# The first block of an attention and feed-forward kernel: four tokens and then three, in place of three and four, with two ReLUs on the vector engine

## The chip, the cores and the metric

The kernel runs on one core of a Trainium2 chip. The metric is the device time of one execution in microseconds; the time of a kernel is the median of several executions. The engines are named as in the profile: PE multiplies matrices, PEld loads its weights, DVE is the vector engine, ACT the scalar (activation) engine, POOL the third elementwise engine, SP an engine that here only issues transfers. All engines take their own instructions in order and wait for one another through semaphores.

## The reference

The inputs are q, k and v, each of 8 batches, 12 heads, 448 positions and 64 values. Attention has a squared ReLU in place of the softmax, and its result goes through a normalised feed-forward layer:

```python
scores = scale * np.matmul(q, k.transpose(0, 1, 3, 2))
attn = np.maximum(scores, 0.0) ** 2 / S
attn_out = np.matmul(attn, v)
x = attn_out.transpose(0, 2, 1, 3).reshape(B, S, H * D)      # d_model = 768
xn = (x - mean(x)) / sqrt(var(x) + 1e-6) * g_ln
out = x + np.maximum(xn @ w_ch1, 0.0) @ w_ch2                # d_ff = 3072
```

## The kernel before

**Tiling.** The 448 positions of a batch are 64 rows of J = 7 positions each; a position within a row is called a token in this text, so one token is 64 columns. A batch is worked through in three groups (n = 0, 1, 2 for batch 0), each of two pairs of heads. Queries and keys are transposed by PE against an identity matrix (`piece`, L250), and DVE or ACT copies the result out of PSUM (L253).

**Blocks.** The queries of batches 0 and 1 are cut into two blocks of tokens, so that the feed-forward layer can start on the first block while attention works on the second. `BLK` (L131) gives the first token and the number of tokens of each block: (0, 3) and (3, 4) for batch 0, (0, 4) and (4, 3) for batch 1. `FEW` (L132) is the size of batch 0's first block. It also sets how the very first loads are cut (L188 to L191): the first FEW tokens of q and k, then the others, on the queues of SP and ACT.

**Scores.** `scores(n, slots, blk)` handles one or two key tokens ("slots") of group n against the block's queries: matmuls of quarter arrays into one PSUM tile (L365; four of them run side by side, each with as many columns as the block has tokens times 64), a ReLU of the tile to bf16 (L376), and a square that is put on the list `later`. `squares_now` (L354) issues the listed squares on DVE. A group has seven slots, so four calls: (0, 1), (2, 3), (4, 5) and (6). With four tokens a tile of two slots has 128 x 1024 elements, with three 128 x 768.

**Values.** `values(n, blk)` multiplies a group's squared scores with its values (L397, 28 matmuls) and DVE scales the sum out of PSUM (L403). `scaled` and `centre` multiply by g (L418, L420), sum over the model dimension on PE (L430), and subtract the mean (L437, six instructions). These tiles and those of the scores come from one pool of three PSUM buffers (`ps_sc`), taken in turn; two more (`ps_mm`) serve the feed-forward layer, fillers and transposes of batch 0.

**The order.** All of it is written out by hand. `first_block` (L549 onwards) runs the first block of batch 0 alone, with fillers (`busy`, `idle`) on PE. Then the feed-forward units of each block (`ffn1_head` L708, `ffn1` L682, each unit six matmuls over the weights w1) are issued between the attention units of the next block: batch 0's first block beside its second, that one beside batch 1's first, and so on. w1 arrives in twelve transfers that POOL issues (L177). `ffn1` gives its ReLU to ACT (L692) or DVE (L690). From about 89 us on come the last units of batch 1 and then the second layer and the other batches, in which no block is cut.

Of the kernel before, what the change touches and what calls it, by code (L numbers as in the profile page):

```python
# [8 lines left out]
ACTF = mybir.ActivationFunctionType  # L9
# [19 lines left out]
def kernel(  # L29
# [22 lines left out]
    nc = tc.nc  # L52
# [9 lines left out]
    J = S // HP  # L62
# [47 lines left out]
    def slots_of(pool, kind, shape, n, o):  # L110

        size = shape[0] * shape[1]
        made = [pool.tile([P, *shape], bf16, tag=f"{kind}{i}", name=f"{kind}_sb", bufs=1) for i in range(n)]
        return made + [spare[:, o:o + size].rearrange("p (a b) -> p a b", b=shape[1])]

    slots = {
        "k": slots_of(io, "k", (2, S), 2, 0),
        "v": slots_of(io, "v", (2, S), 3, 2 * S),
        "kT": slots_of(tpool, "kT", (J, P), 2, 4 * S),
        "qT": slots_of(tpool, "qT", (NB, P), 2, 6 * S)}  # L120
# [7 lines left out]
            return slots[kind][n % 3 if n < LATE else n % 2]  # L128
        return slots[kind][0 if n == G else (n - 2) % 3 if n < LATE else (n + 1) % 2]

    BLK = (((0, 3), (3, J - 3)), ((0, 4), (4, J - 4)))  # L131
    FEW = BLK[0][0][1]  # L132


# [87 lines left out]
    def scale_g():  # L222
        for hf in range(2):
            nc.tensor.matmul(
                idle_ps[hf * HP:(hf + 1) * HP, 1, :K1], g_rows[:, hf], identity_g,
                start=True, stop=True)
        nc.vector.tensor_copy(g_sb, idle_ps[:, 1, :K1])
        nc.vector.tensor_scalar_mul(g_mean, g_sb, -1.0 / d_model)
# [12 lines left out]
    def piece(sb, b, m, n, lo, hi, bank=True):  # L241

        if b == 0 and bank:
            ps = ps_mm.tile([P, 1024], bf16, tag="mm", name="tr_ps")
        else:
            ps = ps_sc.tile([P, 2, 1024], bf16, tag="sc", name="tr_ps")[:, 0]
        src, i = qkv[n, b, m], "qk".index(n)
        for j in range(lo, hi):
            for pr in range(2):
                nc.tensor.transpose(  # L250
                    ps[pr * HP:(pr + 1) * HP, j * P:(j + 1) * P],
                    src[:, pr, j * D:(j + 1) * D], identity)
        return lambda copy, lo=lo, hi=hi: copy(  # L253
            sb[:, i * J + lo:i * J + hi, :], ps[:, lo * P:hi * P].rearrange("p (j c) -> p j c", c=P))
# [76 lines left out]
    FULL = (0, J)  # L331
    FIRST, LAST = (0, BLK[0][0]), (1, BLK[1][1])
    n_early = [0]

    def busy(n):


        ps = ps_mm.tile([P, 512], fp32, tag="mm", name="busy_ps")
        for _ in range(n):
            nc.tensor.matmul(ps[:, :P], ones, ones, start=True, stop=True)  # L340
# [7 lines left out]
    def squares_now(n=None, but=0):  # L348

        if n is None or n in [k for k, _ in later]:
            for _, a in later[:len(later) - but]:
                nc.vector.tensor_mul(a, a, a)  # L354
            del later[:len(later) - but]

    def scores(n, slots, blk, act=False):
        g, w = st[groups[n]], blk[1] * HP
        ps = ps_sc.tile([P, 2, 512], fp32, tag="sc", name="sc_ps")
        for o, i in enumerate(slots):  # L360
            for r in range(2):
                rows = slice(r * HP, (r + 1) * HP)
                for hh in range(2):
                    cols = slice(hh * HP, (hh + 1) * HP)
                    nc.tensor.matmul(  # L365
                        ps[cols, r, o * w:(o + 1) * w], g["k"](i)[rows, cols],
                        g["q"](i, r)[rows, blk[0]:sum(blk), cols], start=True, stop=True)
        if groups[n][0]:
            a = apool.tile([P, 2, 512], bf16, tag="attn", name="attn_sb")
        else:  # L370
            o = n_early[0] % 12 * 1024
            a = early[:, o:o + 1024].rearrange("p (r s) -> p r s", r=2)
            n_early[0] += 1
        since[0] = 0
        a = a[:, :, :len(slots) * w]
        nc.scalar.activation(a, ps[:, :, :len(slots) * w], ACTF.Relu)  # L376
        if act:
            nc.scalar.activation(a, a, ACTF.Square)  # L378
        elif blk == FULL:
            nc.vector.tensor_mul(a, a, a)  # L380
        else:
            later.append((n, a))
        for o, i in enumerate(slots):
            g["attn"].append(a[:, :, o * w:(o + 1) * w])

    def values(n, blk):
        squares_now(n)
        b, m = groups[n]
        v_sb, g, w = qkv["v", b, m], st[groups[n]], blk[1] * HP
        ps = ps_sc.tile([P, 2, 512], fp32, tag="sc", name="av_ps")  # L390
        for j in range(J):
            for hh in range(2):
                rows = slice(hh * HP, (hh + 1) * HP)
                for pr in range(2):
                    cols = slice(pr * HP, (pr + 1) * HP)
                    i, r = g["where"](pr, j)
                    nc.tensor.matmul(  # L397
                        ps[cols, hh, :w], v_sb[rows, pr, j * D:(j + 1) * D],
                        g["attn"][i][rows, r, :], start=(j == 0), stop=(j == J - 1))
        if b // 2 not in xT:  # L400
            xT[b // 2] = xpool.tile([P, K1, S2], bf16, tag="xT", name="xT_sb")
        x = xT[b // 2][:, 2 * m:2 * m + 2, of(blk, b)]
        nc.vector.tensor_scalar_mul(x, ps[:, :, :w], score_scale)  # L403
        g["attn"] = []
        since[0] = 9
        if blk == FULL:
            return
        if b not in xc:
            xc[b] = x_room[:, b]
        if (b, blk) != FIRST:  # L410
            scaled(b, m, blk)

    def scaled(b, m, blk):

        for c in range(2 * m, 2 * m + 2):
            x, y = xT[b // 2][:, c, of(blk, b)], xc[b][:, c, of(blk)]
            if (b, blk) == FIRST:
                nc.scalar.mul(y, x, g_sb[:, c:c + 1])  # L418
            else:
                nc.vector.tensor_scalar_mul(y, x, g_sb[:, c:c + 1])  # L420
# [82 lines left out]
    def transposed(n):  # L503

        if groups[n][0] < by_dma:
            transposes(*groups[n])
            return


        if by_dma * G < n < LATE:  # L510
            load(n + 2, "kq")
        keys_dma(n)
        queries_dma(n)
        if n == LATE + 1:
            put_off.append((n + 2, "kq"))
        elif n >= LATE:
            load(n + 2, "kq")
# [31 lines left out]
    def first_block():  # L549

        blk, sb = BLK[0][0], None
        transposed(0)
        sb = st[0, 0]["sb"]
        scores(0, (0, 1), blk)
        piece(sb, 0, 0, "k", FEW, J)(nc.vector.tensor_copy)
        scale_g()
        busy(3)
        for i in (2, 4, 6):  # L560
            squares_now()
            scores(0, tuple(range(i, min(i + 2, J))), blk)
            busy(3)
        transposed(1)
        squares_now()
        scores(1, (0, 1), blk)
        scores(1, (2, 3), blk)
        busy(3)
        transposed(2)
        squares_now()  # L570
        scores(1, (4, 5), blk)
        held.pop()()
        scores(1, (6,), blk)
        squares_now()
        values(0, blk)
        scores(2, (0, 1), blk)
        busy(3)
        scores(2, (2, 3), blk)
        busy(3)
        scores(2, (4, 5), blk)  # L580
        squares_now(but=2)
        values(1, blk)
        squares_now()
        scores(2, (6,), blk)
        (_, last), = later
        later.clear()
        nc.scalar.activation(last, last, ACTF.Square)
        scaled(0, 0, blk)
        piece(sb, 0, 0, "q", FEW, J, False)(nc.scalar.copy)
        scaled(0, 1, blk)  # L590
        busy(6)
        values(2, blk)
        scaled(0, 2, blk)
        centre(0, blk)
# [586 lines left out]
    def ffn1_units(b, blk):  # L1181
        if (b, blk) == LAST:
            return ([lambda: ffn1_head(b, blk)]
                    + [lambda ni=ni: ffn1_two(b, ni, blk) for ni in range(3, K2 - 1, 2)]
                    + [lambda: ffn1(b, K2 - 1, blk)])
        return [lambda: ffn1_head(b, blk)] + [lambda ni=ni: ffn1(b, ni, blk) for ni in range(3, K2)]
# [36 lines left out]
    pairs = B // 2  # L1223
    narrow = ctx.enter_context(ExitStack())
    first_block()


    units, side = ffn1_units(0, BLK[0][0]), attention_block(0, BLK[0][1])
    units, late = units[:-4], units[-4:]
# [12 lines left out]
    load(8, "qk")  # L1242
    units = ffn1_units(0, BLK[0][1])
    interleave(units[:1] + late + units[1:], attention_block(1, BLK[1][0]), 3)
    fold_tiles()
# [155 lines left out]
```

## Time and profile before

| what | value |
|---|---|
| time, median of 3 runs | 514.17 us (513.85 to 514.24) |
| the profiled execution's own time | 514.53 us |
| its span in the profile | 512.7 us |
| PE busy | 504.5 us, 98% of the span |
| DVE busy | 387.3 us, 76% |
| ACT busy | 309.4 us, 60% |
| POOL busy | 129.6 us, 25% |

Times within the profile count from the start of the span. A line of a timeline or a chain gives the start, the busy time, the engine and the source line, what is written and read, and how many instructions were merged; in brackets it gives the engine's idle time before and what ended it. "sc_ps" are PSUM tiles of scores, "av_ps" of values, "h_ps" of the feed-forward layer, "tr_ps" of transposes; "early" is the room in SBUF in which batch 0's transposed queries and keys and its scores lie. A busy PE is modelled to the end of each matmul's passage through the array, so short idle times of the array do not show.

The early part of the kernel in marks from the trace: the first transposes at 4.60 us, the first scores at 6.07, the first matmul of the feed-forward head of batch 0's first block at 19.51, that of its second block at 37.64, of batch 1's first block at 66.56.

### The profile page before, as it was taken

To read this page: it belongs to the slowest core of one execution; us is meant where nothing else is said; L and a number is where in the kernel's file an instruction comes from. 1 tells how busy PE (TensorE), PEld (TensorE's weight loads), DVE (VectorE), ACT (ScalarE), POOL (GpSimd) and SP (SyncE) were. 2 spreads that over 40 slices of the span, in tenths; PEclk is the share of its full clock that TensorE was granted. 3 is DMA by queue.
4 is the path that set the end of the run, shared out by engine and by line. 5 is a ranking of instruction groups with operands and counts; after the bars stand their busy time and mean duration, and the time that the engine had idled before them with its cause. 6 is when DMAs were issued, how large, how long until landed. Compare 5 with 4: busy or idle time off the path is not lost.

```text
span 512.7 us, 11440 instructions
## 1 busy us (share of the span) xinstructions
PE 504.5 (98%) x4553; PEld 299.0 (58%) x4553; DVE 387.3 (76%) x745; ACT 309.4 (60%) x496; POOL 129.6 (25%) x182
## 2 busy tenths in 40 slices
PE   8899999999999999999999999999999999999996
PEld 6677788855555555555555555555555555556663
DVE  5775765389899888858789968858887968868663
ACT  5966676488678266657757266639979366630000
POOL 8335112012301266321201099501100022200000
PEclk9999999999999999999999999999999999999999
DMA  9999999999969985329995989304997393322222
GB/s 196 206 207 206 211 206 159 158 145 185 190 141 166 185 197 175 130 65 168 187 245 106 186 186 184 94 11 84 188 185 173 71 215 124 94 77 63 63 61 61
DMA packets 124486, 76.31 MB, mean 149 GB/s; under 512 B 80562, under 2 KB 120498, under 8 KB 124434
## 3 DMA queue, kind: packets, MB, share of 16 engines
q1 hardware_dynamic: 93730, 41.38, 39.6%
q0 software_dynamic: 28544, 30.91, 38.3%
q10 hardware_dynamic: 2160, 3.31, 2.8%
q8 instruction: 35, 0.57, 0.5%
q14 instruction: 17, 0.14, 0.1%
HBM read 64.69 MB, written 17.89 MB: 161 GB/s over the span
## 4 chain that ended last, share of the span: by engine, by line
PE 94%; ACT 2%; DVE 1%; DMA 1%; issue 1%; SPq 0%; DVEq 0%
PE m_ps L899 28%; PE o_ps L741 20%; PE o_ps L1109 9%; PE m_ps L1109 8%; PE h_ps L682 8%; PE sc_ps L365 8%; PE av_ps L397 6%; PE h_ps L726 2%; PE h_ps L708 2%; PE o_ps L1071 2%; ACT early L376 1%; PE tr_ps L250 1%; DMA stage_sb<-in_q_dram 1%; DMA out_dram<-o_room 1%; DVE o_room L1125 0%
## 5 line engine op out<-in xcount | busy, mean ns | idle before, releaser
L376 ACT ACTIVATE attn_sb<-sc_ps 128x896 bf16<-128x896 f32 (+4 forms) x150 | 126.3, 902 | 39.4 <-PE sc_ps L365 34.5
L903 ACT ACTIVATE hT_sb<-m_ps 128x448 bf16<-128x448 f32 x144 | 78.2, 543 | 52.0 <-PE m_ps L899 49.3
L741 PE MATMUL o_ps<-w,hT_sb 128*128 128x384 bf16 x624 | 108.3, 327 | 0.0
L741 PEld LDWEIGHTS <-hT_sb 128*128 128x128 bf16 x624 | 58.2, 98 | 45.7 <-issue 10.1
L380 DVE TENSOR_TENSOR attn_sb<-attn_sb 128x896 bf16<-128x896 bf16 x98 | 61.7, 645 | 19.8 <-ACT attn_sb L376 19.1
L682 PE MATMUL h_ps<-x_room,w 128*128 128x256 bf16 (+2 forms) x384 | 43.8, 263 | 0.4 <-ACT early L376 0.3
L1109 PEld LDWEIGHTS <-hT_sb 128*128 128x128 bf16 x312 | 29.7, 98 | 22.1 <-issue 3.0
L980 DVE TENSOR_TENSOR m_ps<-x_room,m_ps 128x448 f32<-128x448 f32 x36 | 22.6, 629 | 23.8 <-ACT hT_sb L903 23.6
L682 PEld LDWEIGHTS <-w 128*128 128x128 bf16 x384 | 33.8, 97 | 7.2 <-issue 2.8
L899 PEld LDWEIGHTS <-w 128*128 128x128 bf16 x246 | 23.9, 97 | 23.1 <-issue 0.4
L1109 PEld LDWEIGHTS <-x_room 128*128 128x128 bf16 x252 | 24.2, 98 | 17.4 <-issue 1.6
L403 DVE TENSOR_SCALAR xT_sb<-av_ps 128x896 bf16<-128x896 f32 (+2 forms) x30 | 27.0, 901 | 9.3 <-PE av_ps L397 9.2
L964 ACT COPY x_room<-m_ps 128x448 f32<-128x448 f32 x36 | 19.1, 531 | 21.6 <-PE m_ps L899 20.7
L899 PEld LDWEIGHTS <-w_sum 128*128 128x128 bf16 x210 | 20.5, 98 | 19.1
L159 POOL DMA_DIRECT2D k_sb<-in_k_dram x15 | 10.7, 712 | 81.1 <-DMA kT_sb<-k_sb 57.3
L899 PE MATMUL m_ps<-x_sum,w 128*128 128x448 bf16 x120 | 29.1, 352 | 0.1
L659 DVE BATCH_NORM_STATS2 stats<-xtok_sb 128x6 f32<-128x384 bf16 x56 | 28.3, 548 | 0.0
L159 POOL DMA_DIRECT2D v_sb<-in_v_dram x20 | 14.2, 711 | 55.5 <-PE sc_ps L365 40.7
L365 PE MATMUL sc_ps<-qT_sb,kT_sb 64*64 64x448 bf16 x392 | 28.2, 358 | 0.0
L692 ACT ACTIVATE hT_sb<-h_ps 128x256 bf16<-128x256 f32 (+1 forms) x49 | 18.0, 368 | 16.1 <-PE h_ps L682 15.2
L378 ACT ACTIVATE attn_sb<-attn_sb 128x896 bf16<-128x896 bf16 x28 | 26.6, 950 | 0.9
L397 PE MATMUL av_ps<-attn_sb,v_sb 64*64 64x448 bf16 (+2 forms) x532 | 26.2, 331 | 0.1
(196 smaller groups left out, 871.7 us busy)
## 6 DMA issues: line engine op xcount, KB each, us to landing
out_dram<-o_room SPq DMA_DIRECT2D x108, 96.0 KB, 2.8
w<-in_moe_w_ch_dram POOLq DMA_DIRECT2D x12, 384.0 KB, 14.3
w<-in_moe_w_ch_dram POOLq DMA_DIRECT2D x4, 1152.0 KB, 20.0
q_sb<-in_q_dram POOLq DMA_DIRECT2D x20, 224.0 KB, 6.2
v_sb<-in_v_dram POOLq DMA_DIRECT2D x20, 224.0 KB, 6.6
k_sb<-in_k_dram POOLq DMA_DIRECT2D x15, 224.0 KB, 6.0
kept<-room SPq DMA_DIRECT2D x4, 480.0 KB, 2.6
kept<-w_sum SPq DMA_DIRECT2D x16, 96.0 KB, 1.7
```

Source lines behind the costliest of these rows:

```text
L365: nc.tensor.matmul(ps[cols, r, o * w:(o + 1) * w], g["k"](i)[rows, cols], g["q"](i, r)[rows, blk[0]:sum(blk), cols], start=True, stop=True)
L376: nc.scalar.activation(a, ps[:, :, :len(slots) * w], ACTF.Relu)
L378: nc.scalar.activation(a, a, ACTF.Square)
L380: nc.vector.tensor_mul(a, a, a)
L397: nc.tensor.matmul(ps[cols, hh, :w], v_sb[rows, pr, j * D:(j + 1) * D], g["attn"][i][rows, r, :], start=(j == 0), stop=(j == J - 1))
L403: nc.vector.tensor_scalar_mul(x, ps[:, :, :w], score_scale)
L659: nc.vector.bn_stats(stats[:, n], xtok[pair][:, n * G:(n + 1) * G, t, :])
L682: nc.tensor.matmul(ps[:, :w + more], w1[:, c, ni * P:(ni + 1) * P], xc[b][:, c, s.start:s.stop + more], start=(c == 0), stop=(c == K1 - 1))
L741: nc.tensor.matmul(ps[:, :DH], hT[pair][:, ki, t * P:(t + 1) * P], w2[:, ki, cols], start=(o == 0), stop=(o == K2 - 1))
L899: nc.tensor.matmul(ps, *at, start=(first and c == 0), stop=(c == KQ - 1), skip_group_check=not first)
L903: nc.scalar.activation(hT[pair][:, n + KH * row, half * S:(half + 1) * S], ps, ACTF.Relu)
L1109: nc.tensor.matmul(ps, x[:, ki], y[ki] if isinstance(y, list) else y[:, ki], start=(first and ki == 0), stop=(ki == KH - 1), skip_group_ch ...
```

## The change

Batch 0's blocks become (0, 4) and (4, 3), the same as batch 1's, and `FEW` with them becomes 4. `scores` gets a parameter with which DVE does the ReLU in place of ACT. `first_block` uses it twice: for slots 4 and 5 of group 0, and for slot 6 of group 1. Line numbers behind L376 move by three.

```diff
-    BLK = (((0, 3), (3, J - 3)), ((0, 4), (4, J - 4)))
+    BLK = (((0, 4), (4, J - 4)), ((0, 4), (4, J - 4)))
     FEW = BLK[0][0][1]
...
-    def scores(n, slots, blk, act=False):
+    def scores(n, slots, blk, act=False, dve=False):
...
         a = a[:, :, :len(slots) * w]
-        nc.scalar.activation(a, ps[:, :, :len(slots) * w], ACTF.Relu)
+        if dve:
+            nc.vector.tensor_scalar_max(a, ps[:, :, :len(slots) * w], 0.0)
+        else:
+            nc.scalar.activation(a, ps[:, :, :len(slots) * w], ACTF.Relu)
...
         for i in (2, 4, 6):
             squares_now()
-            scores(0, tuple(range(i, min(i + 2, J))), blk)
+            scores(0, tuple(range(i, min(i + 2, J))), blk, dve=i == 4)
             busy(3)
...
         held.pop()()
-        scores(1, (6,), blk)
+        scores(1, (6,), blk, dve=True)
         squares_now()
         values(0, blk)
         scores(2, (0, 1), blk)
```

With the new FEW, the first loads of q and k hold four tokens (256 KB each) and the second ones three (192 KB each); in the first block every tile of scores, values, sums and feed-forward outputs of batch 0 is a third wider, and in its second block a quarter narrower. The number of instructions stays the same.

## The prediction

> **What bounds the kernel now.** First the page: the chain of waits by engine, and the busy slices of PE.
>
> ```profile
> PE   8899999999999999999999999999999999999996
> PE 94%; ACT 2%; DVE 1%; DMA 1%; issue 1%; SPq 0%; DVEq 0%
> ```
>
> PE sets the end, except in the first three slices of 12.8 us. Once PE never waits, a delay at the start is a delay at the end, unless PE later waits less or has less to do. So I sum over PE: waits added less waits removed. The windows view places them (columns: length, busy us of PE, PEld, DVE, ACT, POOL, granted clock, DMA share, GB/s).
>
> ```profile
> 4.60:10.20 5.60, 5.01 (x95) 3.31 (x95) 3.42 (x10) 4.15 (x7) 5.57 (x9) 1.00 1.26 215
> 10.20:14.90 4.70, 4.01 (x109) 3.03 (x110) 4.03 (x11) 4.04 (x7) 1.97 (x3) 1.00 1.26 204
> 14.90:19.50 4.60, 4.04 (x104) 3.01 (x104) 2.98 (x8) 4.57 (x11) 1.90 (x3) 1.00 1.24 207
> 21.90:26.10 4.20, 3.85 (x66) 2.86 (x65) 3.24 (x9) 3.76 (x6) 1.37 (x2) 1.00 1.24 207
> 37.60:66.50 28.90, 28.90 (x444) 22.62 (x443) 18.96 (x41) 19.10 (x38) 9.58 (x13) 1.00 1.19 209
> ```
>
> The first block ends at 19.5. In its three windows ACT is 74, 86 and 99% busy, DVE 61, 86 and 65%; PE's 85 to 89% contain fillers that compute nothing. From 37.6 PE is full. The chain in order of time shows who leads in the first block, and where PE waits after it:
>
> ```profile
> 9.83 0.37 DVE early L253
> 10.24 0.61 PE sc_ps L365 x16
> ...
> 12.37 0.81 ACT early L376
> 13.18 0.48 ACT early L253
> 13.66 2.53 ACT early L376 x4
> ...
> 17.98 0.57 DVE xT_sb L403
> ...
> 19.51 2.03 PE h_ps L708 x18
> ```
>
> Copies of transposed keys on DVE release group 1's scores (10.24); then ACT's ReLUs lead to 16.2; a DVE copy leads into the centring. Both engines' queues matter, and the change moves work from one to the other while widening everything. After 19.5 PE has three waits over 0.25 us:
>
> ```profile
> 22.55 0.95 PEld L682 LDWEIGHTS <-w 128*128 128x128 bf16 x12 [0.33 <-issue]
> ...
> 26.12 0.96 PE L397 MATMUL av_ps<-early,v_sb 64*64 64x256 bf16 x28 [0.28 <-ACT early L376]
> ...
> 30.23 0.66 PE L682 MATMUL h_ps<-x_room,w 128*128 128x192 bf16 x6 [0.32 <-ACT early L376]
> ```
>
> The prices, from groups by form (count, busy us, mean ns):
>
> ```profile
> L403 DVE TENSOR_SCALAR xT_sb<-av_ps 128x896 bf16<-128x896 f32 x18 | 19.5, 1086 | 2.6 <-PE av_ps L397 2.6
> L403 DVE TENSOR_SCALAR xT_sb<-av_ps 128x512 bf16<-128x512 f32 x6 | 4.1, 691 | 2.7 <-PE av_ps L397 2.6
> L354 DVE TENSOR_TENSOR early<-early 128x1024 bf16<-128x1024 bf16 x9 | 5.9, 684 | 0.0
> L354 DVE TENSOR_TENSOR early<-early 128x768 bf16<-128x768 bf16 x9 | 4.7, 553 | 0.5 <-ACT early L376 0.4
> L376 ACT ACTIVATE early<-sc_ps 128x1024 bf16<-128x1024 f32 x9 | 8.8, 1019 | 0.7 <-PE sc_ps L365 0.6
> L376 ACT ACTIVATE early<-sc_ps 128x768 bf16<-128x768 f32 x9 | 6.9, 816 | 1.6 <-PE sc_ps L365 1.6
> ```
>
> A ReLU of 1024 on DVE out of PSUM has no row. By the two L403 rows (same form of operation, same source) an element costs (1086-691)/384 = 1.03 ns, so it takes 1.22 us; below it lies the 0.69 of 512, above it 1.37 (twice 0.69). I take 1.22. One of 512 takes 0.69. Work queued back to back starts about 0.09 us before the one ahead has ended (the timeline's starts and ends on DVE; 0.10 on ACT).
>
> **The change part by part.**
>
> *First loads, four tokens in place of three (L191).* q landed at 4.18 and k at 4.52. Bounds: no shift, and in proportion to size, a third of 3.4 us (192 KB took 3.4 and 3.8 us to land, 256 KB 4.3 and 4.6). Between 4.52 and 5.88 another 512 KB landed, 0.34 us for 128 KB; so k +0.34 and q half of it. The other half's loads shrink by as much and land when they did. Cast of k on ACT 0.51 to 0.62, two more transposes and a wider copy (0.36 to 0.42): first scores +0.45, at 6.5.
>
> *Group 0, and DVE's first ReLU.* Two ReLUs of 1019 on ACT from 6.95 end at 8.98, so the square of slots 2, 3 starts at 9.03 (before 8.47). Behind it on DVE: that square (0.68), the new ReLU (1.22), its square (0.68), and only then the key copy that frees group 1's scores: 9.03 + 0.60 + 1.26 + 0.60 + 0.36 = 11.85 (the ReLU with its 0.04 handover). Before, that copy ended at 10.19. The ReLU taken from ACT saves nothing here: ACT had 0.74 us idle before 10.66. Scores of group 1: +1.65, at 11.9. PE's transposes of group 1 are done by then, nothing else is queued on it, and it waits. This is the largest term.
>
> *Groups 1 and 2.* ACT's three ReLUs of group 1 are 0.20 wider each and lose a 0.20 wait: the third ends +2.05, at 15.2. DVE's second ReLU (0.69, slot 6) stands ahead of two squares and of the copy of group 0's values, which frees a PSUM buffer for group 2's slots 4, 5. That copy ended at 14.91. Now DVE runs without a break from the key copies of group 2 (11.68 + 1.6 = 13.3), start to start: copies 0.54 and 0.27, squares 0.60 and 0.60, ReLU 0.60, squares 0.60 and 0.33, the copy itself 0.69: 17.5. So those scores come +2.55. Wider ReLUs and ACT's square (0.2+0.1+0.1+0.1): +3.05 when the last square ends. Values (28 matmuls, 0.19 more), scaling, column sums: the FFN head (L708) starts +3.5, at 23.0; its pace is set by six wider L437 (410 to 479 ns by form), so it ends some +3.95.
>
> *Work that only moved.* 18 matmuls of 256 columns took 1.97 us in the chain, of 192 1.50: 26 ns for 64 columns; a quarter-array one 6.8 (28 took 0.77 and 0.58). Scores and values 168 x 6.8 = 1.14, sums 6 x 26 = 0.16, head 18 x 26 = 0.47: 1.75 us that block two no longer does. So the added wait is 3.95 - 1.75 = **+2.2**.
>
> *Waits that go.* The 0.33 names no engine; weights issued near 9.5 and landing 9.3 to 15.0 us later fit it, and the stage now comes 3.5 us later. The 0.28 and 0.32 are for ReLUs of 1024, now 768 (0.2 less each), behind units 0.16 longer. **-0.9**; bounds -0.5 and -1.3 (with handovers too small for rows).
>
> *Batch 1's first block* (37.6 to 66.5) keeps ReLUs of 1024, but the FFN units between them shrink to 192 columns: 12 matmuls, 0.31 us less per step. At 55 to 60 ACT was 4.62 of 5.00 us busy, and PE's values take the PSUM buffer that a ReLU frees. Two steps have that little room: 0 to +0.6, I take **+0.2**.
>
> *POOL and SP.* POOL's cast of the other query half narrows (0.66, a quarter fewer elements), so the w issues come at most 0.13 earlier into transfers that already share 204 to 215 GB/s: nothing, bounds -0.1 and 0. SP and ACT issue the same four loads.
>
> Sum: +2.2 - 0.9 + 0.2 = **+1.5 us**. The profiled execution took 514.53 (span 512.7), 0.36 over the median; the sum puts it at 516.0, span 514.2, and the median at 515.7.
>
> **Rivals.** (1) *Half of it hides:* DVE's ReLU nearer to ACT's pace (1.02) and later small waits closing bring +0.6, 514.8. For: handovers below 0.1 us are many. Against: the DVE rows are dense and linear. (2) *The other side, faster:* 10 to 37 us is paced by the w transfers (DMA share 1.24 to 1.26 in every window), and PE merely has to be ready as they land. Then the 2.2 is covered, wider tokens give each weight more work, and all handover waits go: up to -1.1, 513.1. It decides if the next block's head (L708, at 37.64) comes less than 1 us later. Against: only one PE wait in that stretch names no engine. (3) *ACT takes over in batch 1:* PE waits at each of three groups for 0.3 to 0.4 us, +1.0 above the forecast, 516.7. For: 4.62 of 5.00. (4) *PE's clock falls back* in the longer waits at 10 and 16 us. At the start 30 fillers took 3.38 us, 113 ns each; six later ones took 0.44, 73 ns. A second slow phase as long as the first (1.1 to 5.4), with PE some four fifths busy, costs up to 2: 1.7, 517.4. Against: the waits are under 2 us, with matmuls between them. That the change does not do what it says is excluded by the built order: DVE holds the two ReLUs.
>
> By the Trainium skill (TensorE: Matmul & The Clock Gate, "What's actually happening") the array falls to half clock after an idle window of about 3.4 us. By that rule the waits here are too short and rival 4 fails; the trace shows two speeds of fillers, while its granted clock reads 1.00 throughout.
>
> **How the numbers follow.** Forecast 0.55 (its own range 514.9 to 516.5), rivals 0.18, 0.09, 0.14, 0.04. What a measurement can tell from no change is 0.2%, 1.03 us: 513.14 to 515.20. Slower: 0.51 of the forecast with rivals 3 and 4, 0.69; faster: rival 2 and 0.01 of rival 1, 0.10; same: what is left of the forecast (0.04) and of rival 1 (0.17), 0.21. From 514.3 to 516.9 leaves out rivals 2 and 4 and the ends of 1 and 3, under 0.2.
>
> **What would show it.** First scores near 6.5; an idle PE before group 1's scores (about 11.9, released by DVE's copy); FFN head near 23.0; no PE wait over 0.25 us from 23 to 41; the next heads near 41.4 and 68.0 in place of 37.64 and 66.5. It is wrong if group 1's scores start before 11, or if the lag of 3.5 us at the first head is not near 1.5 at batch 1's second block.

## The result, and the profile after

| | before | after |
|---|---|---|
| time, median of 4 runs each | 514.04 us (513.85 to 514.24) | 518.20 us (517.73 to 518.36) |
| ratio, 95% interval | | 1.0065 (1.0042 to 1.0088) |
| the profiled execution's own time | 514.53 us | 517.73 us |
| its span | 512.7 us | 515.9 us |
| PE busy | 504.5 us | 506.4 us |

The changed kernel is slower by 4.2 us, and the forecast of 515.7 and its range (up to 516.9) were both too low. The page of the changed kernel, PE's slices, the granted clock's slices, and the chain by engine:

```profile
PE   8899999999999999999999999999999999999996
...
PEclk9999999999999999999999999999999999999999
...
PE 93%; DVE 3%; ACT 1%; issue 1%; DMA 1%; DVEq 0%
```

DVE has 3% of the chain in place of 1%, and PE 93% in place of 94%. In these coarse slices nothing else shows, and the granted clock stands at 9 (90% or more) from the first slice on. The windows of the changed kernel, with the columns used before:

```profile
4.60:10.20 5.60, 5.01 (x60) 2.74 (x61) 2.57 (x7) 3.12 (x4) 5.42 (x9) 1.00 1.26 217
10.20:14.90 4.70, 4.24 (x81) 3.17 (x83) 3.85 (x8) 2.28 (x5) 2.04 (x5) 1.00 1.26 205
14.90:19.50 4.60, 3.41 (x89) 2.44 (x87) 4.60 (x9) 4.23 (x5) 1.93 (x3) 1.00 1.24 206
...
24.70:43.00 18.30, 18.30 (x278) 14.52 (x278) 13.47 (x35) 12.37 (x24) 8.38 (x12) 1.00 1.25 205
43.00:69.60 26.60, 25.92 (x445) 21.23 (x442) 17.94 (x40) 18.35 (x39) 5.72 (x8) 1.00 1.17 210
```

The first line holds the finding. From 4.6 to 10.2 us PE was busy for 5.01 us, to the hundredth as long as before, but it got through 60 matmuls in place of 95. The tiles are only a third wider, and not all of them, so this is more than the change itself explains. The rest is in the timeline of the changed kernel (start, busy us, engine, line, what is written and read, count):

```profile
1.09 3.38 PE L236 MATMUL idle_ps<-ones 128*128 128x128 bf16 x30 [1.09 <-DVE ones L98]
...
4.59 0.46 DVE L199 CAST q_sb<-stage_sb 128x512 bf16<-128x512 f32 x1 [0.99 <-DMA stage_sb<-in_q_dram]
...
5.10 0.64 PE L250 MATMUL tr_ps<-identity,q_sb 128*64 128x128 bf16 x8 [0.63 <-DVE q_sb L199]
...
10.90 1.22 DVE L377 TENSOR_SCALAR early<-sc_ps 128x1024 bf16<-128x1024 f32 x1
10.91 0.50 PE L340 MATMUL busy_ps<-ones 128*128 128x128 bf16 x3
...
13.96 0.34 PE L340 MATMUL busy_ps<-ones 128*128 128x128 bf16 x3
```

Three fillers are the same instruction throughout, 128 columns on constants, with no input to wait for. They take 0.50 us at 10.91 and 0.34 at 13.96. In the kernel before, the change comes much earlier (timeline, same columns):

```profile
5.55 0.34 PE L236 MATMUL idle_ps<-ones 128*128 128x128 bf16 x3
...
6.92 0.34 PE L340 MATMUL busy_ps<-ones 128*128 128x128 bf16 x3
```

In the single records, neighbouring 128-column matmuls start 107 ns apart ahead of the change and 56 ns apart behind it. So PE begins every profiled execution at about half its speed and changes over once. I call that moment the **speed-up**, and read it from the spacing of the records: 5.5 us before, 12.7 us after. The mean granted clock does not show the slow phase, because the record that it is taken from, which lies in the packed traces, begins only at the speed-up: at 5.50 us before, at 12.69 after.

The chain of the changed kernel (start, us, what) shows what stood on the path meanwhile:

```profile
6.76 0.64 PE sc_ps L365 x8
...
11.41 1.55 PE tr_ps L250 x28
...
12.98 0.37 DVE early L253
13.40 0.63 PE sc_ps L365 x16
...
16.95 0.60 DVE early L377
17.55 0.94 DVE early L354 x2
18.49 0.61 DVE xT_sb L406
...
24.66 1.45 PE h_ps L711 x10
```

From group 1's scores on the chain goes where the prediction said, through DVE's second ReLU, squares and copy to group 2. Ahead of them it does not: the copy that releases them (12.98) was to wait for DVE's first ReLU and its square, but the chain reaches it through PE's own transposes of group 1, which run at half speed and end at 12.96. DVE's first ReLU is not on this chain. Group 1's scores come at 13.40 (before 10.24, forecast 11.9) and the head L711 (the old L708) at 24.66 (before 19.51, forecast 23.0). The three later heads lie at 43.09, 69.61 and 90.44 us, and the first matmul of L729, the part behind the last units of batch 1, at 91.94; before, it lay at 88.82. I call this last one **the mark**. From it to the end of the span both took 423.9 us, so that the 3.1 us by which it moved are the 3.1 us of the span. (The medians differ by 4.2 us because the profiled execution of before lay 0.5 us above its median and that of after was the fastest of its four.)

### The profile page after: what moved, and what is told of

Same layout as the page of the kernel before. It is cut to its first block, busy times and chain, and to the rows that moved or that the text cites. A ratio compares the mean times of both kernels' runs of the same rounds, so it can differ in the third digit from the quotient of the medians.

```text
span 515.9 us, 11434 instructions
## 1 busy us (share of the span) xinstructions
PE 506.4 (98%) x4553; PEld 300.6 (58%) x4553; DVE 390.2 (76%) x747; ACT 308.7 (60%) x494; POOL 129.5 (25%) x182
## 4 chain that ended last, share of the span: by engine, by line
PE 93%; DVE 3%; ACT 1%; issue 1%; DMA 1%; DVEq 0%
PE m_ps L902 27%; PE o_ps L744 20%; PE o_ps L1112 10%; PE m_ps L1112 8%; PE sc_ps L365 7%; PE h_ps L685 7%; PE av_ps L400 6%; PE h_ps L729 2%; PE o_ps L1074 2%; PE h_ps L711 1%; ACT attn_sb L379 1%; PE tr_ps L250 1%; DMA stage_sb<-in_q_dram 1%; DVE xT_sb L406 1%; DVE early L354 1%
## 5 line engine op out<-in xcount | busy, mean ns | idle before, releaser
L1112 PEld LDWEIGHTS <-x_room 128*128 128x128 bf16 x252 | 24.2, 98 | 17.3 <-issue 1.6
L695 ACT ACTIVATE hT_sb<-h_ps 128x256 bf16<-128x256 f32 (+1 forms) x49 | 17.9, 366 | 15.6 <-PE h_ps L685 15.0
```

The lines of the kernel that those rows point to most:

```text
L1112: nc.tensor.matmul(ps, x[:, ki], y[ki] if isinstance(y, list) else y[:, ki], start=(first and ki == 0), stop=(ki == KH - 1), skip_group_ch ...
```

## The experiments

Theory **C**: the sum of the prediction holds for an execution with an early speed-up, and the rest of the loss is PE's half speed lasting longer. Rival **W**: the waits in DVE's and ACT's queues are longer than reckoned, whatever PE's speed. After the first four runs C was sharpened to **C2**: PE's speed-up varies from execution to execution, and comes later when PE has idle time among its first matmuls. In the diffs, idle(n) issues n fillers ahead of the first data, and busy(n) fillers between attention steps. Edits are against the changed kernel unless "before" is named. The kernel before ran beside each set of experiments, with medians of 514.30 (a to d), 514.36 (e to h), 514.19 (i, j) and 514.33 us (k, l).

All profiled executions in one table (us from the span's start; "scores 1" are the first scores of group 1):

| kernel | speed-up | first scores | scores 1 | first head | mark | span |
|---|---|---|---|---|---|---|
| before | 5.5 | 6.07 | 10.24 | 19.51 | 88.82 | 512.7 |
| after | 12.7 | 6.76 | 13.40 | 24.66 | 91.94 | 515.9 |
| a: after, 36 fillers | 4.3 | 6.48 | 11.99 | 23.25 | 90.53 | 514.4 |
| b: before, 25 fillers | 3.9 | 5.68 | 9.94 | 19.21 | 88.33 | 512.3 |
| c: new blocks, ACT's ReLUs, 36 | 7.1 | 6.63 | 11.40 | 22.34 | 89.61 | 513.5 |
| d: old blocks, DVE's ReLUs | 6.0 | 6.13 | 10.88 | 20.40 | 89.33 | 513.2 |
| e: after again | 13.6 | 7.33 | 14.07 | 25.32 | 92.58 | 516.5 |
| f: after, slot 6 alone on DVE, 36 | 5.9 | 6.57 | 11.14 | 22.39 | 89.66 | 513.6 |
| g: after, 36, more fillers in group 0 | 6.2 | 6.69 | 12.36 | 23.62 | 90.89 | 516.0 |
| h: before, 33 fillers | 4.0 | 5.54 | 10.00 | 19.26 | 88.35 | 512.4 |
| i: before, 12 fillers | 15.6 | 5.87 | 12.35 | 22.92 | 91.85 | 516.6 |
| j: new blocks, ACT's ReLUs, 30 | 16.7 | 6.75 | 13.49 | 25.73 | 93.01 | 516.7 |
| k: after a third time | 17.3 | 6.72 | 13.46 | 25.91 | 93.18 | 516.9 |
| l: as j | 12.5 | 7.05 | 13.46 | 24.40 | 91.67 | 516.2 |

### a: the changed kernel with six more fillers at the start

```diff
-            idle(30)
+            idle(36)
```

> The changed kernel with 36 fillers on PE at the start in place of 30, so that PE works on until the later queries arrive (5.1 us). Theory C (the clock): the forecast of +1.5 us was right about waits, and the other 1.6 us come from PE running at half speed until 12.6 us in place of 5.5, because it stood idle for 0.8 us before the first transposes; with the gap filled PE should speed up near 5.5 us, first scores near 6.6, group 1's scores near 11.9, the FFN head near 23.1, and the time should fall to about 516.6 us. Theory W (waits only; the slow phase is a matter of chance or covered by waits): the time stays within 0.5 us of 518.2.

Measured: 517.27 us (516.27 to 517.84, 6 runs), ratio 1.0048 (1.0032 to 1.0064). The median lies between the theories. The profiled execution was the fastest of the six, 516.27, and had its speed-up at 4.3 us; from its timeline:

```profile
7.32 0.34 PE L340 MATMUL busy_ps<-ones 128*128 128x128 bf16 x3
...
9.72 1.22 DVE L377 TENSOR_SCALAR early<-sc_ps 128x1024 bf16<-128x1024 f32 x1
...
10.97 0.69 DVE L354 TENSOR_TENSOR early<-early 128x1024 bf16<-128x1024 bf16 x1
...
11.58 0.94 DVE L253 COPY early<-tr_ps 128x384 bf16<-128x384 bf16 x3
11.99 0.63 PE L365 MATMUL sc_ps<-early 64*64 64x256 bf16 x16 [1.68 <-DVE early L253]
```

With PE at full speed the first block behaves as forecast. DVE's ReLU of 1024, its square and the key copies stand one behind the other, PE is idle for 1.68 us waiting for them, and the scores come at 11.99 (forecast 11.9). The heads lie at 23.25, 41.68 and 68.19 (forecast 23.0, 41.4, 68.0) and the span is 514.4 (forecast 514.2). Between this execution and that of the changed kernel above lie 13.40 - 11.99 = 1.41 us at scores 1, 24.66 - 23.25 = 1.41 at the first head, 69.61 - 68.19 = 1.42 at the third and 91.94 - 90.53 = 1.41 at the mark. All of it arises before scores 1, while one of the two runs at half speed, and none afterwards. (This is against a speed-up at 4.3, which is earlier than the 5.5 of before; what that is worth is taken up in the part on the prediction.) The other five executions were slower, four of them by 0.9 us or more, so six fillers do not secure an early speed-up.

### b: the kernel before with five fillers fewer

```diff
 (the kernel before)
-            idle(30)
+            idle(25)
```

> The kernel before with 25 fillers at the start in place of 30: PE idles some 0.8 us ahead of the first transposes, as in the changed kernel, and nothing else differs. Theory C: PE stays at half speed past 5.5 us, to 9 or 12.6 us, and the time rises by 0.4 to 1.9 us (514.5 to 515.9). Theory W: no change within 0.3 us.

Measured: 516.32 us (514.13 to 517.58, 12 runs), ratio 1.0032 (1.0017 to 1.0047). Instructions that compute nothing, ahead of all data, cost 2.0 us at the median when taken away, and executions now spread over 3.5 us. This is against W. The profile caught the fastest of them (speed-up 3.9, mark 88.33), so it does not show the slower ones.

### c: new blocks with both ReLUs on ACT, 36 fillers

```diff
-            idle(30)
+            idle(36)
-            scores(0, tuple(range(i, min(i + 2, J))), blk, dve=i == 4)
+            scores(0, tuple(range(i, min(i + 2, J))), blk)
-        scores(1, (6,), blk, dve=True)
+        scores(1, (6,), blk)
```

> The changed blocks with all ReLUs on ACT and 36 fillers. If DVE's first ReLU is the largest term of the added wait, as forecast (group 1's scores wait behind ReLU and square on DVE), group 1's scores start near 10.9 in place of 11.9 and the time is 0.5 to 1.0 us below that of the run with 36 fillers and the ReLUs on DVE. If ACT is the tighter engine and the ReLUs on DVE help, it is above that run.

Measured: 515.63 us (514.83 to 516.61, 12 runs), ratio 1.0019 (1.0004 to 1.0033). That is 1.6 us below a, more than I had given to the two ReLUs. Scores 1 come at 11.40 against 11.99, although the speed-up was later (7.1 against 4.3). The forecast 10.9 was for an early speed-up.

### d: the old blocks with the two ReLUs on DVE

```diff
-    BLK = (((0, 4), (4, J - 4)), ((0, 4), (4, J - 4)))
+    BLK = (((0, 3), (3, J - 3)), ((0, 4), (4, J - 4)))
```

> The kernel before with blocks of three and four tokens, 30 fillers, and only the two ReLUs moved to DVE (768 and 384 elements). By the forecast's terms DVE's first ReLU (0.15 + 768 x 1.03 ns = 0.95 us) stands ahead of group 1's key copies: group 1's scores start near 11.0 in place of 10.24, and the time rises by 0.4 to 0.9 us; the early loads are those of before, so PE speeds up at 5.5 us. If the moved ReLUs relieve ACT more than they delay the copies, the time falls below 514.0.

Measured: 515.38 us (514.61 to 518.69, 12 runs), ratio 1.0026 (1.0009 to 1.0043): +1.1 at the median. That is above the 0.4 to 0.9 that was expected, though its interval reaches down to them. In the trace scores 1 come at 10.88 (expected 11.0) and the mark is later than before's by 0.51. So DVE's ReLUs cost time with the old blocks too; they take nothing off the path.

### e: the changed kernel, unchanged

> The changed kernel unaltered, to see how its time spreads and when PE speeds up in another execution. Theory C2: the speed-up comes at the end of the first whole window of about 3.4 us in which PE was busy enough, and where the windows lie differs from execution to execution; in the changed kernel most windows before 9 us hold too much idle time, so most executions speed up at 9 to 13 us and take 517 to 518.5, and few come near 516. Rival S (the slow phase seen at 12.7 us was one odd execution): the speed-up comes near 5.5 us here and the time still is 518, so that the missing 1.6 us lie elsewhere.

Measured: 518.04 us (516.95 to 518.96, 6 runs), ratio 1.0056 (1.0035 to 1.0077). The speed-up came at 13.6, late again. The lateness of the first profile was no accident of one execution.

### f: only slot 6's ReLU on DVE, 36 fillers

```diff
-            idle(30)
+            idle(36)
-            scores(0, tuple(range(i, min(i + 2, J))), blk, dve=i == 4)
+            scores(0, tuple(range(i, min(i + 2, J))), blk)
```

> The changed blocks with 36 fillers, DVE doing the ReLU of group 1's slot 6 alone (slots 4, 5 of group 0 back on ACT). If the first ReLU on DVE is the largest term, nearly the whole difference between the two runs with 36 fillers (517.27 with both ReLUs on DVE, 515.63 with none) goes: 515.3 to 516.0, with group 1's scores near 11.0 at an early speed-up. If the second is as dear, the time stays near 516.5.

Measured: 516.22 us (515.24 to 517.80, 12 runs), ratio 1.0026 (1.0012 to 1.0041). With a and c around it this divides the two ReLUs at equal fillers: the one of 1024 in group 0 costs 517.27 - 516.22 = 1.05 us by medians (fastest executions: 516.27 - 515.24 = 1.03), the one of 512 costs 516.22 - 515.63 = 0.59 (0.41). The interval of f overlaps with those of a and c, so this split is an estimate; only the sum, a against c, is nearly clear of noise (their intervals share 0.0001).

### g: more fillers in group 0

```diff
-            idle(30)
+            idle(36)
-            idle(3)
+            idle(6)
-        busy(3)
+        busy(6)
-            busy(3)
+            busy(6)
```

> The changed kernel with both ReLUs on DVE, 36 fillers at the start and six in place of three at the five places of group 0, so that PE is busier up to 10 us. Theory C2: PE then speeds up by 8 us in most executions, the time falls from the 517.3 of 36 fillers alone to 516.0 to 516.5 and spreads less. Rival: PE's idle time does not set the speed-up, the fillers only take PE time, and the time is 517.3 or above.

Measured: 516.81 us (516.32 to 518.99, 12 runs), ratio 1.0034 (1.0016 to 1.0051). That is 0.5 below a, with intervals that overlap, and between the two expectations. The extra fillers cost time of their own: at a speed-up of 6.2 scores 1 come at 12.36, against 11.99 in a. The profiled execution took 425.1 us behind the mark in place of 423.9; the others took 423.7 to 424.8 (i), and I have no cause for these differences.

### h: the kernel before with three fillers more

```diff
 (the kernel before)
-            idle(30)
+            idle(33)
```

> The kernel before with 33 fillers at the start, which closes its gap of 0.3 us ahead of the first transposes. Theory C2: the executions above 515 us that the kernel before shows now and then (7 of 29 so far) become fewer, and the median falls by 0 to 0.3 us. Rival: nothing changes, or the three fillers delay the first transposes by up to 0.1 us.

Measured: 514.29 us (514.02 to 515.71, 12 runs), ratio 0.9993 (0.9980 to 1.0006): no change that can be measured. Two of 12 executions lay above 515 us, against 25 of 93 of the kernel before in all four sets (5 of the first 29, not the 7 that the expectation names). If that saves anything, it is in those few.

### i: the kernel before with 12 fillers

```diff
 (the kernel before)
-            idle(30)
+            idle(12)
```

> The kernel before with 12 fillers at the start: PE is idle from 2.4 us to the first transposes near 4.6, some 2.2 us, so that no window of 3.4 us that ends before 8 us is busy throughout, in any execution. Theory C2: the trace shows half speed (107 ns from one 128-column matmul to the next) to 8 us or later, PE falls behind from the first transposes on as it does in the changed kernel, the FFN head comes 1 to 2 us after 19.5, and the time is 515.0 to 517.5 with few executions below 515. Rival: the speed-up goes by PE's work since the start and not by windows, or fillers do not matter: 514.0 to 514.5.

Measured: 517.82 us (515.59 to 520.46, 7 runs), ratio 1.0060 (1.0034 to 1.0086). This is the decisive run: old blocks, ACT's ReLUs, no edit but the fillers, and it is as slow as the changed kernel. The time lies just above the expected range, and the head at 22.92 came 3.4 us late where 1 to 2 were expected: the direction was right, the effect larger. Its timeline:

```profile
1.09 1.46 PE L236 MATMUL idle_ps<-ones 128*128 128x128 bf16 x12 [1.09 <-DVE ones L98]
4.45 0.53 PE L250 MATMUL tr_ps<-identity,q_sb 128*64 128x128 bf16 x6 [1.90 <-DVE q_sb L199]
...
7.22 0.50 PE L340 MATMUL busy_ps<-ones 128*128 128x128 bf16 x3
...
13.14 0.50 PE L340 MATMUL busy_ps<-ones 128*128 128x128 bf16 x3
```

PE is idle for 1.90 us ahead of the transposes and still slow at 13.14. First scores come at 5.87, earlier than the 6.07 of the profile before, yet scores 1 come at 12.35 in place of 10.24, because the transposes, scores and fillers between them each take longer. The mark is at 91.85; in b, the old blocks with 25 fillers and an early speed-up, it was at 88.33. So 3.5 us lie between two executions whose arithmetic is the same.

### j and l: new blocks with both ReLUs on ACT, 30 fillers

```diff
-            scores(0, tuple(range(i, min(i + 2, J))), blk, dve=i == 4)
+            scores(0, tuple(range(i, min(i + 2, J))), blk)
-        scores(1, (6,), blk, dve=True)
+        scores(1, (6,), blk)
```

> The new blocks with 30 fillers and all ReLUs on ACT: the change without its second part. From the runs with 36 fillers the two ReLUs on DVE cost 0.9 to 1.6 us, so this lies 0.9 to 1.6 us under the changed kernel's 518.0, at 516.4 to 517.1, and above the 515.6 of the same kernel with 36 fillers, since the gap ahead of the first transposes is open again. If the ReLUs on DVE only cost time in the slow phase, it is below 516.

> The new blocks with 30 fillers and all ReLUs on ACT once more. As before half of its executions near 514.7 to 515.2 and the others at 516 to 520; median 515.0 to 516.2.

Measured: j 515.59 us (514.73 to 520.61, 10 runs), ratio 1.0040 (1.0013 to 1.0066); l 517.45 us (514.97 to 518.83, 12 runs), ratio 1.0049 (1.0030 to 1.0068). Both medians missed, one low and one high, because executions fall into early and late ones and the median goes to whichever are more. Together, 22 executions have a median of 516.08. Both profiles happened to be late ones, at 16.7 and 12.5 us.

### k: the changed kernel a third time

> The changed kernel once more, beside the same blocks with all ReLUs on ACT, on one chip in the same call. Up to 9 us the two run the same work, so if only the windows decide when PE speeds up, both have early and late executions in like shares: some of the changed kernel come at 516.2 to 516.8, and the difference of the medians is the price of the ReLUs on DVE alone, 1.0 to 1.6 us. If no execution of the changed kernel is early again (10 of 10 so far above 516.9) while half of the other kernel's are, something besides the gap ahead of the first transposes decides it, and the difference is 2 us or more.

Measured: 518.13 us (516.18 to 519.92, 8 runs), ratio 1.0061 (1.0037 to 1.0086). Two executions, 516.18 and 516.41, are as fast as the early one of a; the profiled one had its speed-up at 17.3 and the latest mark of all, 93.18. The median lies 0.7 us above that of l beside it, under the expected 1.0 to 1.6.

**The parts, put together.** The changed kernel in three sets (18 executions): median 518.1, fastest 516.18. New blocks with ACT's ReLUs, 30 fillers (22): 516.08 and 514.73. The kernel before, all that ran beside them (97): 514.3 and 513.72. The fastest executions, which I take for early ones, give the blocks 514.73 - 513.72 = 1.0 us and the ReLUs 516.18 - 514.73 = 1.45 us, together 2.5. The medians lie 3.8 apart. The 1.3 between I put down to PE's longer time at half speed, which by its times the changed kernel has in most executions and the one before in few. Where the speed-up is late anyway, DVE's ReLUs cost little, 0.2 to 0.3 us at the mark: l against after (12.5 and 12.7) the marks are 91.67 and 91.94, j against k (16.7 and 17.3) 93.01 and 93.18. Scores 1 then wait about as long for PE (13.46 and 13.40; 13.49 and 13.46) whichever engine does the ReLU.

**What decides the speed-up.** The clock record of the packed traces settles more of this than the views. In all 14 profiled executions its stretch at full clock lasts 146, 147, 148 or 149 times 3.413 us, although the speed-ups lie up to 13 us apart: PE's clock changes on a grid of 3.413 us. Laid backwards from each speed-up, the grid gives the windows ahead of it, and the matmul records give the share of each in which the array had columns passing through (128 columns counted as the 107 ns of the slow phase, a matmul on half or a quarter of the array as that share of it). The 14 windows that end at a speed-up come to 77 to 96%. The 26 windows ahead of them, which brought none, come to at most 77%; the closest two are 77.3 and 76.8%. So, as an estimate from these executions, PE speeds up at the end of the first window that is filled to some 77%. In the profile of before the window that ended at 5.50 us held 83%. In that of the changed kernel those that ended at 5.87, 9.28 and 12.69 held 73, 64 and 81%. With 30 fillers the last one starts at 4.16 us and takes columns for 0.107, to 4.26. Up to the first transposes at 5.10 that leaves 0.84 us, so in the changed kernel a window with the whole gap holds at most 75%; up to the 4.60 of before it leaves 0.34 us, and a window can hold 90%. This is how a later load makes a late speed-up likelier. Where the grid lies differs from execution to execution (its first line at 0.3 to 3.3 us), so that executions of one kernel spread.

**What stays open.** The mean granted clock of an execution counts only from its first speed-up on. In the 93 executions of the kernel before that ran beside the experiments it is 0.998 to 1.000. In 6 of the 18 of the changed kernel (517.82 to 518.40 us) it is 0.990 to 0.997, and in 6 more of a, b, j and l it is 0.990 to 0.995. Half clock at the end of the span is too short for that (at most 2.1 us in the traces, 0.002), and 0.990 of 516 us means some 10 us at half speed. The plainest reading is that PE sped up in these executions and then fell back for a while. None of them was profiled, so this is not shown, nor where it happened. It also was not settled why so few executions of the changed kernel are fast: fillers against it (a, g) brought less than the whole.

## Why the prediction was wrong

**The step that failed** is the premise that PE runs at full speed from 5.5 us on, as in the trace of before. *First loads* brings it in ("first scores +0.45, at 6.5"), and *Group 0* rests on it: "PE's transposes of group 1 are done by then, nothing else is queued on it, and it waits". That made DVE's queue alone decide group 1's scores. In the profiled execution PE's slow phase lasted to 12.7, because the later loads left it idle; its transposes of group 1 ended at 12.96, and they led into DVE's copy. Scores 1 came at 13.40 in place of 11.9. The prediction took the end of the slow phase for a fixed time. Against a, which sped up at 4.3, the late speed-up is worth 1.41 of the 3.12 us by which the mark moved. Part of this is that a was earlier than before: in the old blocks a speed-up at 4.0 in place of 5.5 moves the mark by 88.82 - 88.35 = 0.47 (h). So of the 1.6 us that the sum lacked in the trace, an estimated 0.9 are the longer slow phase and 0.7 its other terms. The page's granted clock, which I quoted as 1.00, could not show it. The fillers could: the prediction reads 113 and 73 ns from them, and then uses it for one rival only.

**Rival 4** came nearest: "PE's clock falls back", price 1.7, time 517.4, chance 0.04. Its price and the direction were nearly right (1.4 against a), its mechanism was not that of the profiled execution: PE did not fall back in the waits at 10 and 16 us, at 10 it had not yet sped up. That the price fits is luck there. In the 6 of 18 executions with a mean clock of 0.990 to 0.997 a fall back is likely, so there the rival may hold as written; no trace shows it. "The waits are under 2 us, with matmuls between them" argues against a fall and says nothing on a late rise. By the Trainium skill (TensorE: Matmul & The Clock Gate, "What's actually happening") half clock is the default, and full clock comes only after a busy window of about 3.4 us, sustained, in a window that runs freely and is not reset when the kernel starts. The prediction weighed the idle half of that rule and not this one. The two spacings here (107 and 56 ns), the grid of 3.413 us and the spread of the speed-up agree with it, though its range here, 3.9 to 17.3 us, is far wider than the half microsecond which the Trainium skill gives there. The same section of the Trainium skill has the ramp at under 1% of a typical span; here two kernels that differ only in fillers lie 0.7% apart by it (i against b, 3.5 of 512 us), more than twice what the whole change was forecast to cost.

**Group 0 and DVE's ReLU: right where PE is early.** The groups by form of the changed kernel (count, busy us and mean ns, idle before):

```profile
L377 DVE TENSOR_SCALAR early<-sc_ps 128x1024 bf16<-128x1024 f32 x1 | 1.2, 1218 | 0.0
...
L377 DVE TENSOR_SCALAR early<-sc_ps 128x512 bf16<-128x512 f32 x1 | 0.7, 684 | 0.0
```

The estimate from two rows of other work was 1.22 and 0.69 us. With an early speed-up (a) scores 1 wait for DVE's ReLU, square and copy as said, and come at 11.99. f prices it from outside: without this ReLU on DVE the kernel is 1.05 us faster by the medians and 1.03 by the fastest executions.

**First loads, the size: too small.** q's cast started 0.33 to 0.41 us later than the 4.18 of before in the profiles of a and after (4.51, 4.59), where 0.17 was taken; k's cast 0.35 to 0.41 later than 4.52 (4.87, 4.93), where 0.34 was. q moved by as much as k, not by half of it.

**Groups 1 and 2, the moved work, the waits that go: nearly right in their sum, in part by luck.** At the early speed-up of a the lag against the profile of before is 23.25 - 19.51 = 3.7 us at the first head (forecast 3.5), 41.68 - 37.64 = 4.0 at the second (3.8), and 68.19 - 66.49 = 1.7 at the third (forecast 1.5; the timeline has the third head of before at 66.49, the 66.56 named above is from the chain). But a sped up 1.2 us earlier than before did, which flatters these lags. The waits of 0.28 to 0.33 us on PE are gone: from 24.7 to 43.0 it is busy for 18.30 of 18.30 us.

**Batch 1's first block: too small, just over its bound.** Taken at +0.2, with +0.6 as the bound. PE is busy for 25.92 of the 26.60 us from 43.0 to 69.6, so it waits for 0.68, where it was full before. Two waits show in the timeline of the changed kernel:

```profile
62.39 0.96 PE L400 MATMUL av_ps<-attn_sb,v_sb 64*64 64x256 bf16 x28 [0.28 <-ACT attn_sb L379]
...
65.26 0.64 PE L400 MATMUL av_ps<-attn_sb,v_sb 64*64 64x256 bf16 x12 [0.25 <-DVE attn_sb L354]
```

This is rival 3's mechanism at about half its price. Yet the lag fell by 2.3 us from the second head to the third, as forecast, so something else in that stretch came out about 0.5 us better; no run shows what.

**The other rivals.** Rival 2 (the w transfers pace) fell at the point that it named: the next head came 5.5 us later, not under 1. Rival 1 rested on DVE's ReLU being nearer to 1.02 us, and it took 1.218; something hides only where PE is late anyway (j against k).

**The early price as a whole.** Against an equally early execution of the old blocks (h, 4.0 against a's 4.3) the mark moves by 90.53 - 88.35 = 2.2 us, against the profile of before (5.5) by 1.7; the forecast was 1.5. So even with PE's speed settled the sum was low by 0.2 to 0.7. Against h most of this is there from the first scores on, 6.48 - 5.54 = 0.9 us where 0.45 was taken, for the loads; the first head lags by 4.0 (forecast 3.5) and the second by 41.68 - 37.17 = 4.5 (3.8).

## What to carry to other kernels

A delay in the first microseconds has two prices: the wait itself, and the chance that PE stays slow for longer because the wait left it idle. So before a start-up is changed, PE's speed is read from the spacing of equal fillers in the trace and not from the granted clock, and a kernel whose executions spread is compared by its fastest executions and its marks as well as by its median. Here the granted clock's mean is blind to the slow phase and can show only a later fall. A ReLU moved to an engine that stands between keys and scores is paid in full there as long as PE keeps up, however much idle time that engine has on average.

## What the hardware showed that I had not expected

- The half-speed phase at the start ended between 3.9 and 17.3 us in 14 profiled executions, the same kernel (new blocks and DVE's ReLUs) at 12.7, 13.6 and 17.3; the mean granted clock was 0.998 to 1.000 in every one.
- The speed-up came on a grid of 3.413 us, at the end of the first window in which the array was filled to some 77% (an estimate: 77.3% and more with a speed-up, 76.8% and less without). An idle time of 0.8 us, a quarter of a window, is enough to miss it.
- With 30, 25 and 12 fillers at the start the kernel before took 514.0 to 514.4, 516.3 and 517.8 us: matmuls without any use are worth 3.6 us. With 33 it took 514.3, so that 30 already has nearly all of this.
